# Hash bits of a masked attention kernel by three matmuls per half instead of four, with the two small parts gathered in one tile

## The chip, the cores and the metric

The kernel runs on one core of a Trainium2 chip. The metric is the device time in microseconds (us), from one launch of the program; the number given for a kernel is the median of its runs. The core has a matrix engine (TensorE, in the rows PE, with its weight loads as PEld), a vector engine (DVE), a scalar engine (ACT), GpSimd (POOL), and SP, which here issues every DMA. Each engine works through its own instructions in order and waits at an instruction until its semaphores allow it.

## What is computed

There are three stages. The first is an attention over 2 batches of 8 heads (16 heads), 768 tokens, 64 dimensions, in which a token sees only the tokens of its own hash bucket. The hash of a token has six bits, the signs of six projections of its q or k row:

```python
q_bits = (np.einsum('bhsd,dk->bhsk', q, proj) > 0).astype(np.int64)
k_bits = (np.einsum('bhsd,dk->bhsk', k, proj) > 0).astype(np.int64)
...
mask = q_bucket[:, :, :, None] == k_bucket[:, :, None, :]
scores = scale * np.matmul(q, k.transpose(0, 1, 3, 2))
scores = np.where(mask, scores, -1000000000.0)
...
return np.matmul(attn, v).astype(np.float32)
```

The other two stages are feed-forward blocks on the 1536 rows of 512 columns that the attention gives: `g = h * cos(h)`, then `g = h * tanh(softplus(h))`, each between a 512 to 2048 and a 2048 to 512 matrix.

## The kernel before

Matmuls run on float32 data that is split into a high part (rounded to the matrix engine's fp32r type) and a low part (the rest), and products of the parts are summed. For each head the tile `q2` has 128 rows: the low part of q in rows 0 to 63 and the high part in rows 64 to 127, transposed so that the 768 tokens lie along the row. `k2` is the other way round: high part in rows 0 to 63, low part below. `q1` and `k1` hold the high part in one half and, in the other half, a one-hot code of the hash bucket; so the four matmuls of a score tile (`qk`) give the scores and the mask in one sum.

**The loop.** The attention runs over turns t from -1 on. A turn is one tile of 128 queries of a head, and six turns make one head: `H1, j = divmod(t + 1, J)` with J = 6, so j is the step within the head and H1 counts heads. In a turn the program issues, in this order: the transposes of a probability tile six turns back (`pt(c, 0)`), slot 0, the score matmuls of this turn (`qk(t)`), the exponential of the turn before (`exp(t - 1)`), slot 1, the second group of transposes (`pt(c, 1)`), slot 2, four matmuls with v (`pv`), slot 3. Heads are numbered from 0.

**The slots.** While head H1 is worked on, a table called `plan` places the preparation of head H1 + 1 (and the first half of head H1 + 2) into slots (j, slot): the transposes of q and k (`setup_tr`, whose result ACT copies out of PSUM into q2 or k2), the hash bits (`setup_bits`, one call for each half of 384 tokens: four matmuls into one PSUM tile `wb`, then ACT's Sign into `sg`), and the mask (`setup_mask`: the `match` matmul of `sg` with a code table, then a DVE compare into `oh`, and after the second half two DMAs that copy `oh` into q1 and k1). Head 0 is prepared ahead of the loop in `first_head`, and head 1 has a table of its own, as it is prepared within a single head (t = -1 to 4).

**Four matmuls for the bits.** The weights `prs` hold the projection split in two parts, each for q and for k. A half's bits are q2 times the high part, q2 times the low part, k2 times the high part, k2 times the low part. Since q2 and k2 carry both parts of the data in their 128 rows, each matmul sums both.

**What goes through SP.** All DMAs are on SP's one queue, in program order: the loads of q, k, v of later heads (`load`), of the feed-forward weights (`load_w`), the copies of the high part from q2 to q1 and from k2 to k1 (line 277), of the one-hot rows (lines 302 and 303), and the shift of attention results (`sh`, line 390). Besides, eight completion semaphores are used in turn, so that a DMA is issued only after the one eight places ahead of it has landed.

**PSUM.** The tiles of the transposes, the bits and the match share a pool of three buffers (`ps_w`), the score tiles one of two (`ps_s`): a new score tile waits for the exponential of the tile two turns back.

**Work that fills gaps.** From t = 7 on `fill(j)` puts one piece of the conversion of the first four weight tiles into a turn: ACT pieces at j = 3, DVE pieces (lines 140, 142, 145) at j = 5, 0 and 1, POOL pieces at j = 2. One weight tile takes two heads, so that every second head, up to head 8, has DVE pieces at its j = 0 and j = 1.

## Time and profile before

| what | value |
|---|---|
| time, median of 3 runs | 797.54 us (796.18 to 797.77) |
| the profiled execution's own time | 796.35 us |
| its span, first to last instruction | 794.6 us |
| TensorE busy | 777.2 us (98%), 4020 matmuls |
| VectorE / ScalarE / GpSimd busy | 541.8 / 502.1 / 305.3 us |
| mean granted TensorE clock | 0.994 of full speed |

The profile is of one execution. Busy time of an engine is the time in which at least one of its instructions is recorded as running. Matmuls are pipelined, so a matmul that is recorded with 334 ns can be followed by the next after less than that: the cost of one is read from start to start. Most of the table is an average over three stages with different limits, so the rows below are cut by stage, by head and by step.

### The profile page before, as it was taken

What the parts mean: (1) busy time and instruction counts of PE and PEld (TensorE: products, weight loads), DVE (VectorE), ACT (ScalarE), POOL (GpSimd) and SP (SyncE); (2) the same over time, 40 slices, a digit from 0 to 9 for tenths busy, and PEclk for the clock granted to TensorE, in tenths of its full rate; (3) what the DMA queues carried; (4) which work ended last, traced back from release to release, by engine and by line L of the source; (5) the groups of instructions that cost most, each with busy time, mean ns of one, the idle gap of its engine ahead of it and who ended that gap; (6) DMA issues with size and microseconds to landing.
All of it is one profiled execution on the core that took longest, in us unless ns stands there. A gap on an engine that the chain in (4) does not pass through costs nothing.

```text
span 794.6 us, 11720 instructions
## 1 busy us (share of the span) xinstructions
PE 777.2 (98%) x4020; PEld 665.5 (84%) x4020; DVE 541.8 (68%) x944; ACT 502.1 (63%) x1002; POOL 305.3 (38%) x327
## 2 busy tenths in 40 slices
PE   7999999999999898999999999999999999999998
PEld 5889999999999676887888888888888888888886
DVE  5799899888897898559888546998412766611122
ACT  5899999998997786567777656875223444322120
POOL 4779999998876532102222001232200221200000
PEclk9999999999999999999999999999999999999999
DMA  8454454443320433002332001333100232001011
GB/s 230 105 153 111 105 148 120 105 110 106 85 51 20 139 108 102 30 27 79 107 106 84 23 1 55 105 106 106 54 1 27 81 105 80 1 1 54 0 54 53
DMA packets 38027, 62.36 MB, mean 78 GB/s; under 512 B 3664, under 2 KB 28368, under 8 KB 37968
## 3 DMA queue, kind: packets, MB, share of 16 engines
q1 hardware_dynamic: 37968, 61.63, 26.4%
q8 instruction: 31, 0.51, 0.3%
q14 instruction: 28, 0.23, 0.1%
HBM read 43.13 MB, written 3.15 MB: 58 GB/s over the span
## 4 chain that ended last, share of the span: by engine, by line
PE 59%; DVE 3%; ACT 1%; issue 1%; DVEq 0%; ACTq 0%
PE o L665 30%; PE h L174 29%; DVE hs L199 2%; DVE pa L641 0%; ACT gh L207 0%; ACT hs L184 0%; ACT a L186 0%; DVE gl L209 0%; ACT a L192 0%; DVE ct L142 0%; DVE cg L145 0%; DVE ct L140 0%; ACT pa L627 0%; ACT cg L131 0%; DVE pa L623 0%
## 5 line engine op out<-in xcount | busy, mean ns | idle before, releaser
L174 PE MATMUL h<-xh,w 128*128 128x512 f32 x752 | 246.7, 389 | 0.6 <-POOL xh L397 0.6
L154 POOL TENSOR_TENSOR w<-cg,w 128x512 fp32r<-128x512 f32 x64 | 88.5, 1384 | 343.1 <-ACT w L152 330.9
L209 DVE TENSOR_TENSOR gl<-hs,gh 128x512 fp32r<-128x512 f32 x96 | 69.0, 719 | 168.6 <-ACT gh L207 168.6
L174 PEld LDWEIGHTS h<-xh,w 128*128 128x128 f32 x752 | 141.2, 188 | 30.1 <-POOL xh L397 1.0
L174 PE MATMUL h<-xl,w 128*128 128x512 f32 x376 | 146.4, 389 | 2.3 <-POOL xl L400 2.3
L181 ACT ACTIVATE hs<-h 128x512 f32<-128x512 f32 x48 | 28.7, 598 | 158.7 <-PE h L174 158.7
L665 PE MATMUL o<-gh,w 128*128 128x512 f32 x384 | 120.8, 396 | 4.6 <-DVE pa L625 3.9
L367 DVE TENSOR_TENSOR pl<-wp,ph 128x384 fp32r<-128x384 f32 x192 | 105.8, 552 | 23.3 <-ACT ph L365 22.7
L665 PE MATMUL o<-w,gh 128*128 128x512 f32 x384 | 118.3, 389 | 0.0
L365 ACT ACTIVATE ph<-wp 128x384 fp32r<-128x384 f32 x192 | 95.8, 500 | 17.5 <-PE wp L361 17.4
L326 DVE TENSOR_REDUCE nm<-s 128x1 f32<-128x768 f32 x96 | 90.1, 938 | 5.3 <-PE s L324 5.3
L324 PE MATMUL s<-k,q 128*128 128x512 f32 (+1 forms) x384 | 91.6, 361 | 2.0 <-DVE k L478 1.3
L665 PEld LDWEIGHTS o<-gh,w 128*128 128x128 f32 x384 | 73.4, 192 | 21.1 <-ACT a L192 4.3
L174 PEld LDWEIGHTS h<-xl,w 128*128 128x128 f32 x376 | 70.6, 188 | 17.2 <-POOL xl L400 2.6
L665 PEld LDWEIGHTS o<-w,gh 128*128 128x128 f32 x384 | 72.1, 188 | 15.0
L665 PE MATMUL o<-gl,w 128*128 128x512 f32 x192 | 75.6, 394 | 0.0
L665 PE MATMUL o<-w,gl 128*128 128x512 f32 x192 | 74.7, 389 | 0.0
L377 PE MATMUL u<-ph,nv 128*128 128x384 f32 x192 | 72.5, 378 | 0.0
L184 ACT ACTIVATE hs<-h 128x512 f32<-128x512 f32 x46 | 27.5, 598 | 63.6 <-PE h L174 31.6
L199 DVE SCALAR_TENSOR_TENSOR hs<-hs,b 128x512 f32<-128x512 f32 x48 | 64.9, 1352 | 1.8 <-ACT b L193 1.8
L377 PE MATMUL u<-pl,nv 128*128 128x384 f32 x192 | 64.9, 338 | 0.3 <-DVE pl L367 0.3
L324 PEld LDWEIGHTS s<-k,q 128*128 128x128 f32 x384 | 58.9, 191 | 6.9 <-DVE k L478 1.5
(102 smaller groups left out, 1429.2 us busy)
## 6 DMA issues: line engine op xcount, KB each, us to landing
wr<-in_moe_w_in_dram SPq DMA_DIRECT2D x32, 512.0 KB, 3.8
wr<-in_moe_w_out_dram SPq DMA_DIRECT2D x32, 512.0 KB, 3.3
rq<-in_q_dram SPq DMA_DIRECT2D x16, 192.0 KB, 2.9
rk<-in_k_dram SPq DMA_DIRECT2D x16, 192.0 KB, 2.7
rv<-in_v_dram SPq DMA_DIRECT2D x16, 192.0 KB, 3.4
q<-q SPq DMA_DIRECT2D x16, 192.0 KB, 2.7
k<-k SPq DMA_DIRECT2D x16, 192.0 KB, 2.7
sh<-us SPq DMA_DIRECT2D x32, 96.0 KB, 2.2
```

What stands on the lines that cost most here:

```text
L154: nc.gpsimd.tensor_tensor(w[:, 1], g, f32(w[:, 0]), ALU.subtract)
L174: nc.tensor.matmul(hp, w[:, wi, c, :], X[b][c], start=(i == 0), stop=(i == 3 * NCT - 1))
L181: nc.scalar.activation(hs, hp, ACTF.Mish)
L184: nc.scalar.activation(hs, hp, ACTF.Copy, scale=INV2PI)
L199: nc.vector.scalar_tensor_tensor(hs1, hs1, TWO_PI, b1, ALU.mult, ALU.mult)
L209: nc.vector.tensor_tensor(gl, hs, f32(gh), ALU.subtract)
L324: nc.tensor.matmul(s[:, c0:c1], T[a][:, qs], T[c][:, c0:c1], start=(n == 0), stop=(n == 1))
L326: nc.vector.tensor_reduce(nm, s, AX.X, ALU.max, negate=True)
L365: nc.scalar.activation(ph, w, ACTF.Copy)
L367: nc.vector.tensor_tensor(pl, w, f32(ph), ALU.subtract)
L377: nc.tensor.matmul(U[0], lw, x, start=(kt == 0 and n == 0), stop=(kt == J - 1 and n == 1))
L665: nc.tensor.matmul(O[d], lhs, rhs, start=(first and x == 0), stop=(last and x == 2))
```

## The change

The two matmuls with the low part of the projection are replaced by one. Its moving operand is a new tile `z`, 128 rows by 768 tokens, which holds the high part of q in rows 64 to 127 and the high part of k in rows 0 to 63; its weights `prz` hold the low part of the projection for k in rows 0 to 63 and for q in rows 64 to 127. The product of the two low parts is left out. A half's bits are then q2 and k2 with the high weights, and z with `prz`. The tile z is filled by DMAs on SP, one for each side and each half of the tokens, issued right behind ACT's copy of that part; the two copies into q1 and k1 move behind them, to the place of the last one. Head 0 keeps its four matmuls.

`sg` becomes one buffer of a half's size, written by each half in turn; so the second half's bits move from slot (2, 1) to (3, 1), behind the match of the first half. For head 1 the table changes to bits at (2, 3) and (3, 2) (before: (2, 1) and (2, 3)), mask at (3, 1) and (4, 1) (before: (3, 1) and (3, 3)). `prw`, a source of the weights, takes a turn in the pool of raw weight tiles in place of a tile of its own, so that the third weight load of `first_head` also waits for the last of POOL's two new instructions that make `prz`.

```diff
-    prw = persist.tile([128, 2, 128], F32, name="prw")
     prs = persist.tile([128, 2, 2, 128], F32R, name="prs")
+    prz = persist.tile([128, 128], F32R, name="prz")
...
                 o = T[a][:, half * HF:half * HF + HF]
                 nc.scalar.activation(o, tr_unit(nat_t[h], half), ACTF.Copy, scale=sc)
+                if half == 0 and side == 0:
+                    T["z"] = oh_p.tile([128, S], F32R, tag="z", name="z")
+                cs = slice(half * HF, half * HF + HF)
+                nc.sync.dma_start(out=f32(T["z"][rows:rows + 64, cs]), in_=f32(T[a][rows:rows + 64, cs]))
                 if half == 1:
-                    nc.sync.dma_start(out=f32(T[b][64:128, :]), in_=f32(T[a][rows:rows + 64, :]))
+                    if side == 1:
+                        nc.sync.dma_start(out=f32(T["q1"][64:128, :]), in_=f32(T["q2"][64:128, :]))
+                        nc.sync.dma_start(out=f32(T["k1"][64:128, :]), in_=f32(T["k2"][0:64, :]))
                     nat_t.pop(h)
...
-                for i, (x, nm, part) in enumerate((x, nm, part) for x, nm in enumerate(("q2", "k2")) for part in range(2)):
-                    nc.tensor.matmul(w, prs[:, part, x, :], T[nm][:, cs], start=(i == 0), stop=(i == 3))
-                if half == 0:
-                    T["sg"] = oh_p.tile([128, S], F32R, tag="sg", name="sg")
-                nc.scalar.activation(T["sg"][:, cs], w, ACTF.Sign, bias=tiny, scale=1.0)
+                if h:
+                    ws = ((prs[:, 0, 0, :], "q2"), (prs[:, 0, 1, :], "k2"), (prz, "z"))
+                else:
+                    ws = [(prs[:, part, x, :], nm) for x, nm in enumerate(("q2", "k2")) for part in range(2)]
+                for i, (lw, nm) in enumerate(ws):
+                    nc.tensor.matmul(w, lw, T[nm][:, cs], start=(i == 0), stop=(i == len(ws) - 1))
+                if h or half:
+                    sg = oh_p.tile([128, HF], F32R, tag="sg", name="sg")
+                else:
+                    sg = p_p.tile([128, S], F32, tag="p7", name="sg0")[:, 0:HF].bitcast(F32R)
+                T["sg", half] = sg
+                nc.scalar.activation(sg, w, ACTF.Sign, bias=tiny, scale=1.0)
...
+                nc.gpsimd.tensor_tensor(prz[0:64, :], prw[0:64, 1], f32(prs[0:64, 0, 1]), ALU.subtract)
+                nc.gpsimd.tensor_tensor(prz[64:128, :], prw[64:128, 0], f32(prs[64:128, 0, 0]), ALU.subtract)
...
-                        (1, 1): lambda: setup_bits(h, 0), (2, 1): lambda: setup_bits(h, 1),
+                        (1, 1): lambda: setup_bits(h, 0), (3, 1): lambda: setup_bits(h, 1),
...
-                        (2, 1): lambda: setup_bits(h, 0), (2, 3): lambda: setup_bits(h, 1),
-                        (3, 1): lambda: setup_mask(h, 0), (3, 3): lambda: setup_mask(h, 1),
+                        (2, 3): lambda: setup_bits(h, 0), (3, 2): lambda: setup_bits(h, 1),
+                        (3, 1): lambda: setup_mask(h, 0), (4, 1): lambda: setup_mask(h, 1),
```

Where the change moves instructions is seen best in an engine's list. The first place is SP's queue at the start of the loop, where head 1 is prepared. Before, from the last of the loads that `first_head` and the first turn issue (`rq`, `rk`, `rv`: q, k, v of later heads) to the one-hot copies of head 1 (`q_263`, `k_265` are q1 and k1 of head 1, `q_264`, `k_266` its q2 and k2; DMAHW0 to 7 are the eight completion semaphores):

```order
L247 DMA rq<-in_q_dram 128x384 [waits DMAHW0_49,Pool_49]
L247 DMA rk<-in_k_dram 128x384 [waits DMAHW1_49,Pool_49]
L247 DMA rv<-in_v_dram 128x384 [waits DMAHW2_49,Pool_49]
L277 DMA q_263<-q_264 64x768 [waits DMAHW3_49,Activation_49]
L277 DMA k_265<-k_266 64x768 [waits DMAHW4_49,Activation_49]
L302 DMA q_263<-oh 64x768 [waits DMAHW5_49,DVE_49]
L303 DMA k_265<-oh 64x768 [waits DMAHW6_49]
```

The same place now (`q_267`, `k_269` are q1 and k1 of head 1, `q_268`, `k_270` its q2 and k2):

```order
L247 DMA rq<-in_q_dram 128x384 [waits DMAHW0_49,Pool_49]
L247 DMA rk<-in_k_dram 128x384 [waits DMAHW1_49,Pool_49]
L247 DMA rv<-in_v_dram 128x384 [waits DMAHW2_49,Pool_49]
L279 DMA z<-q_268 64x384 [waits DMAHW3_49,Activation_49]
L279 DMA z<-k_270 64x384 [waits DMAHW4_49,Activation_49]
L279 DMA z<-q_268 64x384 [waits DMAHW5_49,Activation_49]
L279 DMA z<-k_270 64x384 [waits DMAHW6_49,Activation_49]
L282 DMA q_267<-q_268 64x768 [waits DMAHW7_49]
L283 DMA k_269<-k_270 64x768 [waits DMAHW0_49]
L315 DMA q_267<-oh 64x768 [waits DMAHW1_49,DVE_49]
L316 DMA k_269<-oh 64x768 [waits DMAHW2_49]
```

Four transfers into z stand between the loads and the copies; the copies of the high part and of the one-hot rows come four places later.

The second place is TensorE in the same stretch, from the second score tile of head 0 on. Before (`s` are score tiles, `wb` the bits, `wm` the match; `q_264` and `k_266` are q2 and k2 of head 1):

```order
L324 MATMUL s<-k_183,q_181 128x256
L285 MATMUL wb<-q_264,prs 128x384 [waits Activation_49]
L285 MATMUL wb<-q_264,prs 128x384
L285 MATMUL wb<-k_266,prs 128x384 x2
L285 MATMUL wb<-q_264,prs 128x384 [waits Activation_49]
L285 MATMUL wb<-q_264,prs 128x384
L285 MATMUL wb<-k_266,prs 128x384 [waits Activation_49]
L285 MATMUL wb<-k_266,prs 128x384
L324 MATMUL s<-k_182,q_180 128x512 [waits Activation_49]
```

Now, at the same place:

```order
L337 MATMUL s<-k_186,q_184 128x256
L295 MATMUL wb<-q_268,prs 128x384 [waits Activation_49]
L295 MATMUL wb<-k_270,prs 128x384
L295 MATMUL wb<-z,prz 128x384 [waits DMAHW4_49,DMAHW3_49]
L337 MATMUL s<-k_185,q_183 128x512 [waits Activation_49]
L337 MATMUL s<-k_185,q_183 128x256
L337 MATMUL s<-k_186,q_184 128x512
L337 MATMUL s<-k_186,q_184 128x256
L305 MATMUL wm<-sg,code 128x384 [waits Activation_49]
L295 MATMUL wb<-q_268,prs 128x384 [waits PE_49]
L295 MATMUL wb<-k_270,prs 128x384
L295 MATMUL wb<-z,prz 128x384 [waits DMAHW6_49,DMAHW5_49]
```

The third matmul of each half now waits for two transfers into z, and the third score tile of head 0 stands behind the first of these waits; the second half's bits stand behind that score tile and the first match.

The third place is TensorE in a later head, at j = 2 and j = 3. Before, from the score tile of j = 2 on, the second half's bits stand at j = 2, ahead of the second transposes (`wp`):

```order
L324 MATMUL s<-k_2347,q_2345 128x256
L285 MATMUL wb<-q_2642,prs 128x384 [waits Activation_49]
L285 MATMUL wb<-q_2642,prs 128x384
L285 MATMUL wb<-k_2644,prs 128x384 x2
L361 MATMUL wp<-con,hs 128x128 [waits DVE_49]
```

Now they stand one step later, behind the score tile of j = 3, and j = 2 has none:

```order
L337 MATMUL s<-k_2383,q_2381 128x256
L295 MATMUL wb<-q_2682,prs 128x384 [waits DVE_49]
L295 MATMUL wb<-k_2684,prs 128x384
L295 MATMUL wb<-z,prz 128x384 [waits DMAHW1_49,DMAHW0_49]
L374 MATMUL wp<-con,hs 128x128 [waits DVE_49]
```

Each half has one matmul less, and the first waits on DVE, through the PSUM buffer that it takes over, where it waited on ACT.

## Rows read from the trace of the kernel before

**Rows 1.** Windows: us; busy PE, PEld, DVE, ACT, POOL (instructions); clock; DMA share, GB/s.

```profile
0.00:24.14 24.14, 18.81 (x104) 14.20 (x104) 11.55 (x25) 13.84 (x28) 14.06 (x26) 0.93 0.76 210
57.85:238.90 181.05, 181.05 (x1274) 171.12 (x1272) 165.30 (x398) 167.38 (x390) 163.82 (x192) 1.00 0.41 107
```

**Rows 2.** Timeline of TensorE, one step of head 10: start, us, operation.

```profile
163.21 0.94 PE L324 MATMUL s<-k,q 128*128 128x512 f32 x4
163.99 0.51 PE L285 MATMUL wb<-q,prs 128*128 128x384 f32 x2
...
164.69 0.27 PE L361 MATMUL wp<-con,hs 128*128 128x128 f32 x1
...
178.27 0.48 PE L324 MATMUL s<-k,q 128*128 128x512 f32 x1
```

**Rows 3.** Busy time by engine of two heads, from j = 2 to j = 2; columns as Rows 1.

```profile
103.01:118.06 15.05, 15.05 (x109) 14.24 (x108) 13.98 (x35) 14.18 (x33) 14.88 (x19) 1.00 0.54 141
...
163.21:178.27 15.06, 15.06 (x110) 14.27 (x108) 13.33 (x33) 13.70 (x33) 13.84 (x18) 1.00 0.40 107
```

**Rows 4.** Single steps: j = 1, 2, 3 with conversion pieces, then j = 2 without.

```profile
130.36:133.11 2.75, 2.75 (x21) 2.59 (x19) 2.75 (x7) 2.64 (x7) 2.75 (x4) 1.00 0.71 164
133.11:136.04 2.93, 2.93 (x22) 2.78 (x21) 2.93 (x8) 2.63 (x6) 2.93 (x4) 1.00 0.91 268
136.04:138.27 2.23, 2.23 (x18) 2.11 (x17) 2.23 (x6) 1.89 (x5) 2.23 (x4) 1.00 0.51 177
...
178.27:181.20 2.93, 2.93 (x22) 2.77 (x21) 2.27 (x6) 2.64 (x6) 2.17 (x3) 1.00 0.64 221
```

**Rows 5.** Timeline of DVE: one conversion piece in those steps.

```profile
133.80 0.68 DVE L145 SCALAR_TENSOR_TENSOR cg<-cg,ct 128x512 int32<-128x512 int32 x1
```

**Rows 6.** Loads of line 247 at 11.2 to 13.3 us: last issue, time to landing.

```profile
L247 SPq DMA_DIRECT2D rv<-in_v_dram x1: 459/459/459, 12.8 to 12.8; - x1
...
DMA to landing us min/median/max: 7.9/8.3/8.6
```

**Rows 7.** Copies of line 277 at 14.9 to 17 us: issues, time to landing.

```profile
L277 SPq DMA_DIRECT2D q<-q x1: 467/467/467, 15.0 to 15.0; - x1
L277 SPq DMA_DIRECT2D k<-k x1: 467/467/467, 16.4 to 16.4; - x1
...
DMA to landing us min/median/max: 6.5/6.8/7.2
```

**Rows 8.** The last one-hot copy of head 1, line 303: issue, time to landing.

```profile
L303 SPq DMA_DIRECT2D k<-oh x1: 589/589/589, 18.3 to 18.3; - x1
...
DMA to landing us min/median/max: 5.6/5.6/5.6
```

**Rows 9.** Timeline of TensorE while head 1 is prepared.

```profile
13.34 0.51 PE L285 MATMUL wb<-q,prs 128*128 128x384 f32 x2
...
21.50 1.61 PE L324 MATMUL s<-k,q 128*128 128x512 f32 x4
...
24.14 1.03 PE L324 MATMUL s<-k,q 128*128 128x512 f32 x4
```

**Rows 10.** DMA issues by kind: count, KB, median us to landing.

```profile
sh<-us SPq DMA_DIRECT2D x32, 96.0 KB, 2.2
...
k<-oh SPq DMA_DIRECT2D x15, 192.0 KB, 3.0
```

**Rows 11.** Timelines of ACT and TensorE: k2's first half of a head, then its bits.

```profile
172.98 0.52 ACT L275 ACTIVATE k<-wt 128x384 fp32r<-128x384 f32 x1
...
176.28 0.34 PE L285 MATMUL wb<-q,prs 128*128 128x384 f32 x1
```

**Rows 12.** Busy time by engine at 22 to 26 us; columns as Rows 1.

```profile
22.00:26.00 4.00, 4.00 (x24) 3.73 (x23) 1.98 (x5) 3.45 (x9) 3.79 (x6) 0.71 0.32 68
```

**Rows 13.** Groups of instructions: busy us, mean ns of one, idle time before.

```profile
L326 DVE TENSOR_REDUCE nm<-s 128x1 f32<-128x768 f32 x96 | 90.1, 938 | 5.3 <-PE s L324 5.3
...
L298 DVE TENSOR_SCALAR oh<-wm,con 128x384 fp32r<-128x384 f32 x30 | 20.0, 668 | 0.0
```

More of the change, by code (lines that the diff above doesn't have):

```diff
@@ L283, in setup_bits @@
                 w = ps_w.tile([128, HF], F32, tag="w", name="wb")
-                for i, (x, nm, part) in enumerate((x, nm, part) for x, nm in enumerate(("q2", "k2")) for part in range(2)):
-                    nc.tensor.matmul(w, prs[:, part, x, :], T[nm][:, cs], start=(i == 0), stop=(i == 3))
-                if half == 0:
-                    T["sg"] = oh_p.tile([128, S], F32R, tag="sg", name="sg")
-                nc.scalar.activation(T["sg"][:, cs], w, ACTF.Sign, bias=tiny, scale=1.0)
+                if h:
[10 more added lines that the diff above has]
+                nc.scalar.activation(sg, w, ACTF.Sign, bias=tiny, scale=1.0)
             def match(h, half):
                 w = ps_w.tile([128, HF], F32, tag="w", name="wm")
-                nc.tensor.matmul(w, code, tt[h]["sg"][:, half * HF:half * HF + HF])
+                nc.tensor.matmul(w, code, tt[h]["sg", half])
                 return w
@@ L426, in attention @@
             nc.vector.memset(warm, 0.0)
+            prw = raw_p.tile([128, NCT, 128, 2], I32, tag="w", name="prw").bitcast(F32)[:, 0].rearrange("p (x f) t -> p x (f t)", x=2)
             nc.gpsimd.memset(prw, 0.0)
```

## Prediction

> **What bounds the kernel now.** I cut the table of windows by stage first. The reader is to see two attention stages, not one. From 57.85 to 238.90 us TensorE is recorded as busy in all of 181.05 us at full clock; up to 24.14 us it is busy for 18.81 us only, while the DMA engines are busy for 0.76 of the time [rows 1]. So the long stretch is bound by TensorE, and the start by something else.
>
> Whether a busy TensorE is one that works without a stall is read from its timeline, by starts. In head 10 a score tile starts at 163.21 us and the one six turns later at 178.27 us [rows 2], a period of 15.05 us that the two heads shown share to 0.01 us [rows 3]; the four matmuls of a half's bits take from 163.99 to 164.69 us [rows 2], 0.175 us each from start to start. Nothing in that is a wait.
>
> The other engines have little room in the same period. In a head with conversion pieces DVE is busy for 13.98 and ACT for 14.18 of 15.05 us, and POOL for 14.88 us; later, without pieces, 13.33, 13.70 and 13.84 us [rows 3]. Cut by step it is tighter: from j = 1 to j = 3 of a head with pieces DVE has no idle time at all (2.75, 2.93 and 2.23 us busy of as much), where the same j = 2 without pieces leaves it 0.66 us of 2.93 [rows 4]. The piece of line 145 alone is 0.68 us [rows 5].
>
> Then the start, in SP's queue. The loads issued from 11.3 to 12.8 us land 7.9 to 8.6 us later, so the last one, of v, at 12.8 + 8.6 = 21.4 us [rows 6]. What is issued behind lands behind: the copy q2 to q1 of head 1 goes out at 15.0 and lands 7.2 us later at 22.2, that of k2 goes out at 16.4 and lands 6.5 us later at 22.9 [rows 7], and the last one-hot copy goes out at 18.3 and lands 5.6 us later at 23.9 [rows 8]. The first score tile of head 1 starts at 24.14 us [rows 9], right behind it. But the hash bits of head 1 ran already from 13.34 us on [rows 9]: they needed no transfer, and the mask, the score tiles of head 0 and the one-hot copies were all done or issued while the queue emptied. That is the cover which I look at below.
>
> **What the change removes.** One matmul for each half of heads 1 to 15: 30 in all. For head 1 it falls into a stretch in which TensorE waits anyway. For the 14 others it is 2 x 0.175 = 0.35 us of a period of 15.05, at most 14 x 0.35 = 4.9 us. At the other bound it is nothing, where another engine sets the pace of the steps. Which it is I take head by head. DVE does the same work as before. In the heads with pieces at j = 0 and j = 1 (heads 2, 4, 6 and 8, four of the fourteen) it is busy through j = 1, 2 and 3 without a break [rows 4], and its lead or lag against TensorE is held by three PSUM buffers; the bits at j = 2 were the time in which it caught up, and they move away. There I take no gain. In the other ten DVE was idle for 0.66 us in j = 2 [rows 4], and 0.70 us of bits now comes one step later, at j = 3, where 0.52 us of it is left; so it loses no room ahead of the tight steps, and I take the full 0.35. Sum: 10 x 0.35 = 3.5 us, with bounds of 1.75 (half of that, if a new wait appears in every second head) and 4.9.
>
> **What it adds to a steady head.** Four transfers of 96 KB. One of that size lands in 2.2 us by the median [rows 10]. The closest is k's first half: ACT's copy out of PSUM ends at 172.98 + 0.52 = 173.50, and the bits start at 176.28 [rows 11], the third matmul 0.35 us later; 173.50 + 0.47 for the issue (the duration of such an issue in [rows 7]) + 2.2 is 176.2, so 0.45 us are left. If it landed as the slower copies do, in 3.0 us [rows 10], TensorE would lose 0.35 us per head, all of the gain. I cost it at nothing, since the size is that of the 2.2 us row. The copies into q1 and k1 go out later, but are read a step and more later than the one-hot copies; the queue time of four issues (4 x 0.47 = 1.9 us of 15) leaves SP waiting most of the time. POOL's two small instructions, and the third weight load's wait on them, come ahead of the loop, where POOL has the loads still to wait for that land up to 21.4 us [rows 6]; without that cover they would cost less than 1 us, once.
>
> **What it adds at the start.** Here the cover is gone. The four transfers into z for head 1 stand behind the loads that land up to 21.4 us [rows 6]. Two copies of 192 KB land 0.7 to 0.8 us apart there [rows 7], so a transfer of half the size takes some 0.4 us: the first two, which the first half's bits need, have landed at 21.4 + 2 x 0.4 = 22.2 us. TensorE works in order. It reaches that third matmul at 13.34 + 0.35 = 13.7 us and waits there for 8.5 us; queued behind are the third to sixth score tile of head 0, the matches, and the transposes for head 2, none of which needs z. Followed on:
> - 22.2: third matmul. TensorE's clock will be low after this idle time: before, at 22 to 26 us, the granted clock was 0.71 on average, that is partly at 1.2 GHz, after shorter gaps, and a score tile at 21.50 took 1.61 us [rows 12, 9] where one takes 0.94 [rows 2]. So the bits end at 22.5 and the next score tile's last matmul near 24.1.
> - Then the first match and the second half's three matmuls, at about 0.35 us each at the low clock as far as it lasts: 24.9.
> - The next score tile, whose buffer must have been read by an exponential that stood behind the first Sign, 0.94 and some latency: 25.9. Its maximum on DVE, which stands ahead of the second half's mask, 0.94, and the mask 0.67 [rows 13]: 27.5.
> - The two one-hot copies, issued 0.47 us apart [rows 7]; the second lands 3.0 us after its issue [rows 10], in a queue that is now empty: 31.0.
>
> Head 1's first score tile then starts at 31.05 instead of 24.14: a loss of 6.9 us, that nothing gives back, since TensorE is the bound behind it. Bounds: with the full clock throughout 0.7 (a score tile) and 0.7 (bits and match) go away, 5.5; with the low clock for two more score tiles 1.1 come on top, 8.0.
>
> **The sum.** 6.9 - 3.5 = 3.4 us more than the profiled execution's own 796.35 (794.6 of span and 1.75 around it): 799.75. That execution is 1.2 us below the median of the three runs; taking half of that gives 800.4 us.
>
> **Rivals.**
> - *The start costs nothing (faster).* TensorE waited in this stretch before too, for POOL and ACT, and ended with the one-hot copies at 23.9; if the transfers into z from SBUF overtook the loads, or the rest of head 1's preparation fitted into the old waits, only the gain is left: 796.35 - 3.5 to - 4.9, near 792.5. It decides from the point where z's first half lands before 15 us. Against it: all of four copies issued there landed behind the loads, in order [rows 6 to 8].
> - *z pays its own duration only.* If a transfer took 2.2 us [rows 10] from its issue, as one into an empty queue, the second would go out at 16.4 [rows 7], land at 18.6, and the chain above would end 3.6 us earlier: a loss of 3.3, and with the gain of 3.5 a time of 796.2, no change. The copies of the same place, with 6.5 and 7.2 us, speak against it. The Trainium skill (DMA: Bandwidth & Descriptors, Anatomy of one DMA) gives a fixed 2.0 us and the bytes at 436 GB/s for each DMA, a fit from GpSimd's path; for 96 KB that is an estimate of 2.2 us, which the 2.2 us of [rows 10] bears out and the start does not.
> - *Another engine takes the whole gain.* POOL's 14.88 us in a head [rows 3] is more than the new period of 14.70, or z comes late at j = 1 in each head (0.35 us each, above). Then the loss stands alone: 796.35 + 6.9, near 803.3. Against it: POOL's work in the other heads is 13.84, and its results are used turns later.
>
> **How the numbers follow.** My forecast, a start that costs 5.5 to 8.0 and a gain of 1.75 to 4.9, has 0.67; the first rival 0.14, the second 0.11, the third 0.08. The forecast's own range is 796.35 + 0.6 to + 6.25, with up to 1.2 for the median: 797.0 to 803.8. For 8 in 10 I go from 796.2 to 803.8, which takes in the second rival and leaves out the first and some of the third. About 0.2% (1.6 us) is what a measurement can tell from no change: slower than that is most of the forecast (0.58 of its 0.67) and the third rival, 0.66; the same is the rest of the forecast and most of the second rival, 0.19; faster is the first rival and a little of the second, 0.15.
>
> **What would show it.** Right: TensorE idle for some 8 us up to 22 us, ended by a DMA into z; head 1's first score tile near 31 us; then periods of 14.70 us, with about 15.05 in heads 2, 4, 6 and 8; the end of the attention 3 to 4 us later. Wrong: z landing ahead of the loads; a first score tile of head 1 before 27 us; periods that are not shorter in the heads without pieces; or waits for z at j = 1 of every head.

## The result and the profile after

The changed kernel takes 802.58 us, the median of 5 runs (800.26 to 803.64), against 797.54 us: the ratio is 1.0063 with a 95% interval of 1.0041 to 1.0084. It is slower, by about 5 us (0.6%). The profiled execution took 803.14 us (span 801.3, granted clock 0.989); the one of the kernel before took 796.35 us (span 794.6). TensorE has the 30 matmuls less (3990) and is busy for 775.7 us. The line numbers are those of the changed kernel now: 337 the score tile, 295 the bits, 305 the match, 279 the copies into z.

The start answers to [rows 9]. The timeline of TensorE while head 1 is prepared (start, us, operation, idle time before it and what ended it; rows left out are marked with dots):

```profile
13.55 0.34 PE L295 MATMUL wb<-q,prs 128*128 128x384 f32 x1
13.73 0.33 PE L295 MATMUL wb<-k,prs 128*128 128x384 f32 x1
21.26 0.66 PE L295 MATMUL wb<-z,prz 128*128 128x384 f32 x1 [7.20 <-DMA z<-k]
21.71 1.48 PE L337 MATMUL s<-k,q 128*128 128x512 f32 x4
...
24.27 1.45 PE L337 MATMUL s<-k,q 128*128 128x512 f32 x4
...
31.11 0.47 PE L337 MATMUL s<-k,q 128*128 128x512 f32 x1 [1.52 <-DMA k<-oh]
```

The first two matmuls of the bits run where they ran before; the third stands for 7.20 us until z has landed. Head 1's first score tile comes at 31.11 us, 6.97 us later than in [rows 9]. 0.2 us of that were there before the preparation: head 0's first score tile came at 11.25 us, in the profile before at 11.05.

SP's queue answers to [rows 6, 7]. The last load, and the four copies into z (issues, then the time from issue to landing):

```profile
L247 SPq DMA_DIRECT2D rv<-in_v_dram x1: 432/432/432, 13.0 to 13.0; - x1
...
DMA to landing us min/median/max: 7.4/7.4/7.4
```

```profile
L279 SPq DMA_DIRECT2D z<-q x2: 468/508/547, 15.0 to 17.0; - x2
L279 SPq DMA_DIRECT2D z<-k x2: 467/512/558, 16.4 to 17.6; - x2
...
DMA to landing us min/median/max: 4.2/4.6/5.8
```

The load issued at 13.0 lands at 20.4. The first copy into z lands at 15.0 + 5.8 = 20.8 and the last at 17.6 + 4.2 = 21.8, in order behind it; the second, which completes the first half of z, lands at 21.1.

The heads and steps answer to [rows 1, 3, 4]. Windows of the changed kernel: the stretch that was all TensorE, then head 10, then j = 1, 2 and 3 of head 4 (with conversion pieces), then j = 3 of head 5 (without); columns as Rows 1.

```profile
57.85:238.90 181.05, 180.01 (x1262) 167.02 (x1261) 164.99 (x399) 168.62 (x395) 167.74 (x197) 1.00 0.53 137
167.54:182.25 14.71, 14.71 (x107) 13.78 (x106) 13.24 (x32) 13.56 (x34) 14.04 (x17) 1.00 0.53 135
...
77.05:79.64 2.59, 2.59 (x20) 2.42 (x19) 2.59 (x7) 2.56 (x6) 2.59 (x4) 1.00 0.51 116
79.64:81.97 2.33, 2.33 (x18) 2.04 (x17) 2.33 (x7) 2.13 (x5) 2.33 (x4) 1.00 0.95 278
81.97:85.16 3.19, 3.05 (x22) 2.52 (x20) 3.19 (x8) 2.58 (x6) 3.19 (x4) 1.00 0.90 237
...
97.10:99.88 2.78, 2.78 (x22) 2.51 (x20) 2.78 (x8) 2.44 (x6) 2.78 (x4) 1.00 0.45 131
```

Head 10 has a period of 14.71 us, as forecast. But TensorE is no longer recorded as busy all the time: in head 4 the step from 81.97 us (j = 3), which now holds the second half's bits, takes 3.19 us where the same step of head 5 takes 2.78. All periods, first score tile to first score tile, for the kernels that matter below (us, good to 0.01; each from the timeline of its one profiled execution; the kernels of the last three columns are those of the next section):

| head | before | changed | head 1 old | bits at j = 2 | pieces moved |
|---|---|---|---|---|---|
| 1 | 14.87 | 14.73 | 16.61 | 17.00 | 14.67 |
| 2 | 16.07 | 16.38 | 16.37 | 16.07 | 15.39 |
| 3 | 15.07 | 14.83 | 14.87 | 14.90 | 14.97 |
| 4 | 15.04 | 15.22 | 15.24 | 14.98 | 14.77 |
| 5 | 15.05 | 14.73 | 14.72 | 14.83 | 14.98 |
| 6 | 15.05 | 15.12 | 15.16 | 14.98 | 14.71 |
| 7 | 15.06 | 14.73 | 14.92 | 15.31 | 15.88 |
| 8 | 15.04 | 15.97 | 15.99 | 15.37 | 14.71 |
| 9, 10 | 15.06, 15.05 | 14.72, 14.71 | 14.70, 14.73 | 14.75, 14.74 | 14.70, 14.72 |
| 11, 12 | 15.06, 15.05 | 14.92, 14.72 | 14.71, 14.73 | 14.75, 14.73 | 14.70, 14.73 |
| 13, 14 | 15.06, 14.12 | 14.71, 13.81 | 14.71, 13.77 | 14.75, 13.79 | 15.56, 13.77 |

From head 1 to head 14 the changed kernel wins 1.33 us in all, not 3.5. From head 2 on TensorE never waits for z in this execution.

Two more places cost time. In head 8 POOL stood idle ahead of the addition that needs the transfer `sh`; that transfer, issued at 142.3 us, landed 5.4 us later, at 147.6, right behind a weight load of 512 KB that was issued ahead of it:

```profile
L403 SPq DMA_DIRECT2D sh<-us x1: 467/467/467, 142.3 to 142.3; - x1
...
DMA to landing us min/median/max: 5.4/5.4/5.4
```

```profile
147.71 1.01 POOL L407 TENSOR_TENSOR xt<-us,sh 64x384 f32<-64x384 f32 x1 [1.89 <-DVE pl L380]
148.68 0.99 POOL L257 TENSOR_TENSOR nk<-rk,nk 128x384 fp32r<-128x384 f32 x1
```

```profile
149.73 0.45 PE L263 MATMUL wt<-ident_r,nk 128*128 128x128 f32 x3 [0.62 <-POOL nk L257]
```

The view names DVE as what ended POOL's wait, since a `pl` ended at the same moment. But the addition starts 0.07 us behind the landing, as the additions of heads 2, 4 and 6 that wait for `sh` do, so the landing is what it waited for. Behind the addition stands k's low part, and TensorE waits for that: the step takes 3.15 us instead of 2.29. In the kernel before, the `sh` of the same place took 4.7 us too and cost nothing: it went out 3.7 us behind the head's first score tile, and now 5.4 us behind it. So most of the delay is the later issue.

And behind the attention TensorE's granted clock is 0.50 (the 1.2 GHz level) for twice as long. First the kernel before at that place, then the changed kernel:

```profile
300.81:304.23 3.42, 3.13 (x8) 2.49 (x9) 3.28 (x7) 1.85 (x4) 0.09 (x1) 0.50 0.05 12
```

```profile
305.46:312.28 6.82, 5.54 (x13) 4.41 (x14) 6.67 (x10) 3.22 (x6) 1.60 (x1) 0.50 0.27 83
```

The lag against the kernel before grows there from 5.64 to 6.76 us. So the profiled executions add up: 6.97 (start) - 1.33 (heads) + 1.1 (clock) = 6.7 us, the difference of the two spans.

### The profile page after: what moved, and what is told of

Its sections match the earlier page's. It is cut to its first block, busy times and chain, and to the rows that moved or that the text cites. A ratio compares the mean times of both kernels' runs of the same rounds, so it can differ in the third digit from the quotient of the medians.

```text
span 801.3 us, 11825 instructions
## 1 busy us (share of the span) xinstructions
PE 775.7 (97%) x3990; PEld 660.6 (82%) x3990; DVE 541.8 (68%) x944; ACT 501.4 (63%) x1002; POOL 305.3 (38%) x329
## 3 DMA queue, kind: packets, MB, share of 16 engines
HBM read 43.13 MB, written 3.15 MB: 58 GB/s over the span
## 4 chain that ended last, share of the span: by engine, by line
PE 59%; DVE 3%; ACT 1%; issue 1%; DVEq 0%; ACTq 0%
PE o L681 30%; PE h L174 29%; DVE hs L199 2%; DVE pa L657 0%; ACT gh L207 0%; ACT hs L184 0%; ACT a L186 0%; DVE gl L209 0%; ACT a L192 0%; DVE ct L142 0%; DVE cg L145 0%; DVE ct L140 0%; ACT pa L643 0%; ACT cg L131 0%; DVE pa L639 0%
## 5 line engine op out<-in xcount | busy, mean ns | idle before, releaser
L184 ACT ACTIVATE hs<-h 128x512 f32<-128x512 f32 x46 | 27.5, 598 | 64.8 <-PE h L174 32.8
```

The source lines that it names most:

```text
L184: nc.scalar.activation(hs, hp, ACTF.Copy, scale=INV2PI)
```

## The experiments

Times are medians; "before" is the kernel before, measured beside each group on the same chip: 797.09 us beside the first four kernels, 797.72 us beside the next seven, 797.97 us beside the last. The first eight kernels ran on one chip, the next three on a second and the last on a third, so across these groups the ratios are the better measure. Each kernel was profiled in one execution. Only the lines of an edit that matter most are shown; the same condition also switches the transfers into z.

**Head 1 as before, the rest changed.**

```diff
-                if h:
+                if h and not (h == 1):
                     ws = ((prs[:, 0, 0, :], "q2"), (prs[:, 0, 1, :], "k2"), (prz, "z"))
...
-                        (2, 3): lambda: setup_bits(h, 0), (3, 2): lambda: setup_bits(h, 1),
-                        (3, 1): lambda: setup_mask(h, 0), (4, 1): lambda: setup_mask(h, 1),
+                        (2, 1): lambda: setup_bits(h, 0), (2, 3): lambda: setup_bits(h, 1),
+                        (3, 1): lambda: setup_mask(h, 0), (3, 3): lambda: setup_mask(h, 1),
```

> The changed kernel, but head 1 is prepared as before: four matmuls for each half, the old places in its table, no transfers into z for it. My theory (the start costs 6.9 us because z of head 1 waits behind the loads, and everything else is worth -1.3 us): head 1's first score tile starts at 24.1 us again, the heads keep the periods of the changed kernel (14.7, and 15.1 to 15.4 in heads 2, 4, 6 and 8), and the time is 795.0, or up to 796.2 if the second stretch at the low clock behind the attention lasts 6.8 us here too. Rival (the 6.9 us are not lost through z but turn up wherever the queue is held back): first score tile at 24.1, but the lag comes back within heads 1 to 3, and the time is 800 or more.

Measured: 796.1 us (795.20 to 798.13), ratio to before 0.9983 (0.9971 to 0.9996), so 6.5 us below the changed kernel. Head 1's first score tile starts at 24.35 us, and from head 2 to head 14 the periods are those of the changed kernel within about 0.2 us (third column of times). Only head 1 itself lost 1.7 us against the kernel before, and not through the queue: the clock stayed at 0.50 for 6.8 us there:

```profile
22.24:29.06 6.82, 6.31 (x27) 5.34 (x26) 3.51 (x8) 4.75 (x11) 5.24 (x7) 0.50 0.76 203
```

In the profile before, the low clock lasted 3.4 us there, from 20.92; the kernel with the pieces moved, further down, has the same start, no low clock at all there, and 14.67 us for head 1. So the 6.9 us sit in the preparation of head 1, and the rest of the change is worth a little more than 1 us.

**Only head 1 changed.**

```diff
-                if h:
+                if h and not (h > 1):
                     ws = ((prs[:, 0, 0, :], "q2"), (prs[:, 0, 1, :], "k2"), (prz, "z"))
...
-                        (1, 1): lambda: setup_bits(h, 0), (3, 1): lambda: setup_bits(h, 1),
+                        (1, 1): lambda: setup_bits(h, 0), (2, 1): lambda: setup_bits(h, 1),
```

> Only head 1 has the three matmuls, the transfers into z and the new places; heads 2 to 15 have four matmuls, the bits of both halves at j = 1 and j = 2, and the copies where they were. My theory: head 1's first score tile at 31.1, then 15.05 us per head as before, so the time is 796.35 + 6.9 = 803.3. Rival (the lag of the start is given back later, since buffers are fuller or DVE has caught up): below 800.

Measured: 804.81 us (803.52 to 804.95), ratio 1.0081 (1.0064 to 1.0099). The third matmul waits 7.07 us for z and head 1's first score tile starts at 31.65:

```profile
21.70 0.66 PE L298 MATMUL wb<-z,prz 128*128 128x384 f32 x1 [7.07 <-DMA z<-k]
31.65 0.59 PE L344 MATMUL s<-k,q 128*128 128x512 f32 x2 [1.60 <-DMA k<-oh]
```

The lag is 7.52 us at head 1 (0.76 of it are there at head 0's first score tile already) and 7.57 at the last score tile: nothing is given back. Another 1.0 us comes behind the attention, again with 6.8 us at the low clock; that and the later start of head 0 make up most of what this execution took above the 803.3 us that I expected.

**The move alone: four matmuls, second half's bits at j = 3.**

```diff
-                if h:
+                if h and not (h > 0):
                     ws = ((prs[:, 0, 0, :], "q2"), (prs[:, 0, 1, :], "k2"), (prz, "z"))
```

> Four matmuls in every head and no z; only the place of the second half's bits is the new one (j = 3 instead of j = 2) and sg has one half's size; head 1 has its old table. My theory (in heads 2, 4, 6 and 8 the moved bits wait for DVE, which has no idle time from j = 1 to j = 3): heads without conversion pieces keep 15.05 us, heads 2, 4, 6 and 8 take some 0.2 us more, since TensorE comes there 0.17 us later than with three matmuls; time 796.35 + 0.8 = 797.2. Rival (the stall at j = 3 belongs to z, whose last transfer lands too late for the second half): no stall, 15.05 us in every head, 796.4.

Measured: 799.07 us (796.16 to 802.54), ratio 1.0029 (1.0010 to 1.0047). Heads 6 and 8 take 15.21 us each, heads 5, 7 and 9 to 14 what they took before: 0.16 us more, about the theory's 0.2, and no z is there to cause it. The total is more than forecast, since heads 1 to 4 lose 3.7 us in the profiled execution; 2.4 of that lies in heads 3 and 4, where DVE's conversion pieces ran beside other POOL work (last section).

**Second half's bits back at j = 2, with three matmuls.**

```diff
-                        (1, 1): lambda: setup_bits(h, 0), (3, 1): lambda: setup_bits(h, 1),
+                        (1, 1): lambda: setup_bits(h, 0), (2, 1): lambda: setup_bits(h, 1),
...
-                    sg = oh_p.tile([128, HF], F32R, tag="sg", name="sg")
+                    sg = oh_p.tile([128, HF], F32R, tag="sg", name="sg", bufs=2)
```

> Three matmuls and z from head 2 on, head 1 as before, and the second half's bits at j = 2 as before, with two sg buffers of half size (the low projection weights of heads 0 and 1 stand in a probability tile that is not yet in use). My theory (the move to j = 3 makes the stalls in heads 2, 4, 6 and 8): these heads take 14.9 to 15.05 us, the others 14.7, and the time is 796.35 - 3.3 to - 4 = 792.4 to 793.0, or a microsecond more if the low clock behind the attention lasts as in the changed kernel. Rival (DVE is short in these heads wherever the bits stand): the same stalls of 0.4 us, and the time of the kernel that has only head 1 as before.

Measured: 796.76 us (793.95 to 798.34), ratio 0.9983 (0.9967 to 0.9998): the same as with the bits at j = 3. I had expected 792.4 to 793.0, and missed. Both theories have a part of it. Heads 4 and 6 go from 15.2 to 14.98 us, so the move does cost 0.2 us there; but they don't reach 14.7, and heads 7 and 8 now take 15.3 to 15.4 us. In the profile the low clock of the start, 6.8 us again, takes 2.1 us more of head 1 than in the kernel before (17.00 against 14.87 us).

**The weight loads issued later.** The three loads of 512 KB that `first_head` puts into SP's queue go to three turns of the loop. This edit was tried on the changed kernel, on the kernel before, and on the one with head 1 as before:

```diff
-                for _ in range(3):
-                    load_w()
...
+                if t in (4, 10, 16):
+                    load_w()
```

> The changed kernel with one more edit: the three weight loads of 512 KB that stand ahead of head 1's loads in SP's queue are issued later, one each at t = 4, 10 and 16. My theory (z of head 1 takes 5 to 6 us since it lands behind 1.5 MB of weights and the loads after them): the transfers into z land some 2.2 us after their issue, the third matmul of the first half starts near 18.7 instead of 21.3, head 1's first score tile near 28.4 instead of 31.1, and the time is 2.7 us less than the changed kernel's 802.6: near 800. Rival (the transfers within SBUF are slow there by themselves, or the wait is for POOL): third matmul at 21.3 as before, 802.6.

Measured on the changed kernel: 796.5 us (795.25 to 797.65), 6 us less, ratio to before 0.9985 (0.9975 to 0.9996). The direction was right and the size twice what I expected: SP issues a DMA only after the one eight places ahead has landed, which for the first two copies into z were weight loads (landed at 14.91 and 16.37, copies issued at 14.97 and 16.43), so that without these the copies also go out 1.7 to 2.6 us earlier. The copies into z, and TensorE:

```profile
L279 SPq DMA_DIRECT2D z<-q x2: 467/506/546, 13.3 to 14.5; - x2
L279 SPq DMA_DIRECT2D z<-k x2: 547/547/547, 13.8 to 15.1; - x2
...
DMA to landing us min/median/max: 2.1/2.2/2.5
```

```profile
16.12 0.41 PE L295 MATMUL wb<-z,prz 128*128 128x384 f32 x1 [1.84 <-DMA z<-k]
...
24.80 0.47 PE L337 MATMUL s<-k,q 128*128 128x512 f32 x1 [1.83 <-DMA k<-oh]
```

They land in 2.1 to 2.5 us instead of 4.2 to 5.8. That is the transfer's own time, and the wait shrinks from 7.20 to 1.84 us. The queue is shown as the cause of most of the wait.

> The kernel before with the same edit of the weight loads and nothing else. My theory: its last one-hot copy of head 1, which landed 5.6 us after its issue, lands in about 3.0 us, but TensorE waits in that stretch for POOL too (the transposes of k of head 2 started at 21.1 behind a wait for POOL), so that head 1's first score tile comes 0.5 to 2.5 us earlier than 24.1; time 796.6 to 794.6. Rival (the queue was hidden in the kernel before, POOL alone sets the end of head 0): 24.1 and no change.

Measured on the kernel before: 795.75 us (794.55 to 796.82), ratio 0.9982 (0.9971 to 0.9992). Head 1's first score tile starts at 22.43 instead of 24.14. The queue was not fully hidden there either. Against this kernel, the changed one with late loads is still 2.4 us behind at that tile and 0.75 us slower by the medians. No run separates what of that is z's own transfer and what the later places of head 1's bits and masks.

> Head 1 prepared as before (four matmuls, no z), the rest as in the changed kernel, and the three weight loads issued at t = 4, 10 and 16. My theory: the saving of the kernel that has only head 1 as before (1.3 us of periods against the kernel before, some of it lost to a longer stretch at the low clock at the start) and that of the late loads add up: 0.5 to 2.5 us less than without late loads, 793.5 to 795.5. Rival (POOL alone sets the end of head 0): the time of the kernel with only head 1 as before, 796.1.

Measured with head 1 as before: 794.48 us (792.99 to 794.84), ratio 0.9963 (0.9951 to 0.9975); first score tile at 22.00. The two savings add up: 0.9983 times 0.9982 is 0.9965.

**DVE's pieces moved.** Head 1 as before, and:

```diff
-            SLOTS = {"A": (3,), "D": (0, 1, 5), "P": (2,)}
+            SLOTS = {"A": (3,), "D": (0, 4, 5), "P": (2,)}
```

> Head 1 prepared as before, the rest as in the changed kernel, and DVE's conversion pieces moved from j = 5, 0 and 1 to j = 4, 5 and 0. My theory (in heads 2, 4, 6 and 8 TensorE waits at j = 3 for DVE, which has no idle time from j = 0 to j = 3 there, while j = 4 leaves it 0.6 us): heads 4 and 6 take 14.7 instead of 15.1 to 15.2 us, head 8 keeps its other stall of 0.8 us if that is the queue's; time about 1.2 us below the kernel with only head 1 as before, near 795. Rival (the stall at j = 3 comes from the later bits themselves): heads 4 and 6 stay at 15.1 to 15.2 us, 796.1.

Measured: 795.3 us (794.01 to 797.8), ratio 0.9975 (0.9960 to 0.9991). Heads 4, 6 and 8 take 14.77, 14.71 and 14.71 us: the step with the second half's bits is 2.77 us in heads 6 and 8, as in heads without pieces. The stall belonged to DVE. The pieces have a smaller price at their new place: heads 3, 5 and 7 take 0.25 us more at j = 0, as they do in the kernel before with both edits below. The time itself is not clear of that without the move (0.9983, 0.9971 to 0.9996), and its profile also lacked the low clock at the start, which is worth 1.9 us of head 1; the argument rests on the steps. Head 8's other stall went too; its weight load now stands one step earlier in the queue. New ones appeared in head 7 (15.88 us) and head 13 (15.56), where k's first half of z was late; head 7:

```profile
L280 SPq DMA_DIRECT2D z<-k x1: 461/461/461, 112.0 to 112.0; - x1
...
DMA to landing us min/median/max: 3.9/3.9/3.9
```

```profile
115.96 0.44 PE L298 MATMUL wb<-z,prz 128*128 128x384 f32 x1 [0.64 <-DMA z<-k]
```

**Both edits together,** on three kernels: with head 1 as before, on the whole change, and on the kernel before.

> Head 1 as before, three matmuls from head 2 on, the three weight loads issued at t = 4, 10 and 16, and DVE's conversion pieces at j = 4, 5 and 0: the two edits together. My theory (the queue of the start and DVE in heads 2, 4, 6 and 8 are separate places): head 1's first score tile near 22, heads 4, 6 and 8 at 14.7 to 14.8 us, time near 793 (794.5 of the kernel with late loads, less some 1.5 of stalls). Rival (transfers into z that land late now and then give the rest back): some heads with a stall of 0.6 to 0.9 us at j = 0, and 794.5.

> The whole change, head 1 included, with the late weight loads and the pieces at j = 4, 5 and 0. My theory: the transfers into z of head 1 still put 2 us into the start even with the queue empty (24.8 instead of 22.0 for head 1's first score tile with late loads), so the time is some 2 us above the same kernel with head 1 as before: near 795. Rival (with the queue empty z costs nothing): equal to it, 793.

> The kernel before, four matmuls and old places, with the same two edits: late weight loads, pieces at j = 4, 5 and 0. My theory (the kernel before has no wait for DVE in heads 4, 6 and 8, only some in head 2): 0 to 1 us below the kernel before with late loads alone, 794.8 to 795.8; so that three matmuls from head 2 on, with head 1 as before, are worth 1.8 to 2.8 us in the same surroundings. Rival (the edits, not the three matmuls, made the faster times): the same time as with three matmuls, 793.

Measured: 793.57 us (792.87 to 794.9; ratio 0.9948, 0.9930 to 0.9965), 795.41 us (793.37 to 799.04; ratio 0.9971, 0.9953 to 0.9989), and 795.31 us (794.61 to 795.68; ratio 0.9973, 0.9965 to 0.9982). The first is the fastest kernel of the study, 0.5% below the kernel before. In the same surroundings three matmuls from head 2 on are worth 795.31 - 793.57 = 1.7 us (the two intervals just touch), and taking head 1 into the change costs 1.8 us even with the queue empty (first score tile at 24.58 instead of 22.77). The intervals of the first and the second of these kernels overlap, but the tile says the same. So the whole change with both edits is no faster than the kernel before with both edits.

In the first, the rival had a part too. Heads 7 and 13 keep their late z (15.95 and 15.31 us), head 4 did not come down (15.23 us; TensorE waits for `pl` again), and in head 2 (16.51 us) a z that was queued behind two of the late weight loads held TensorE up:

```profile
45.17 0.41 PE L298 MATMUL wb<-z,prz 128*128 128x384 f32 x1 [0.91 <-DMA z<-k]
```

**The first half's bits later,** on the fastest kernel:

```diff
-                        (1, 1): lambda: setup_bits(h, 0), (3, 1): lambda: setup_bits(h, 1),
+                        (1, 3): lambda: setup_bits(h, 0), (3, 1): lambda: setup_bits(h, 1),
```

> The kernel with head 1 as before, late weight loads and pieces at j = 4, 5 and 0, and now the first half's bits behind the v matmuls of j = 1 instead of ahead of the second transposes there. My theory (single transfers into z land 3.5 to 4.3 us after their issue instead of 2.1, and where that is k's first half TensorE waits 0.6 to 1.2 us at the bits of j = 1, as in heads 7 and 13): the bits come some 0.8 us later, heads 7 and 13 lose 0.1 us or nothing, and the time is about 1 us less than without this edit, near 792.5. Rival (the first half's sign and match are then late, and TensorE waits at the match of j = 2 in every head): each head takes 0.1 us more, 795 or above.

Measured: 796.64 us (793.57 to 797.91), ratio 0.9978 (0.9962 to 0.9993). The rival won, though through another wait than it named. The late z of head 7 no longer costs anything (15.41 us), but from head 3 to head 14 every step with the second half's bits takes 3.17 to 3.19 us. The waits of these twelve heads (who waited for whom, us in total, times, longest), then, in head 10, where no piece is near, DVE and TensorE:

```profile
PEld wb L298 <- DVE pl L383: 5.4, 12, 0.5
```

```profile
164.49 0.94 DVE L342 TENSOR_REDUCE nm<-s 128x1 f32<-128x768 f32 x1
165.35 0.55 DVE L383 TENSOR_TENSOR pl<-wp,ph 128x384 fp32r<-128x384 f32 x1
```

```profile
164.87 0.94 PE L340 MATMUL s<-k,q 128*128 128x512 f32 x4
165.95 0.45 PE L298 MATMUL wb<-q,prs 128*128 128x384 f32 x1
```

The bits start right behind DVE's `pl`, which ends at 165.90 and sets free the PSUM buffer.

## Why the prediction was right, and where it was off

**The bound, and the cover at the start: right.** TensorE's order, the transfers into z behind the loads, and what stands behind the third matmul came as forecast. So did the steady heads' transfers into z, which I had costed at nothing: TensorE never waited for one there. Step by step: the two transfers of the first half landed at 21.1 us (forecast 22.2), the first half's bits then released TensorE, the last but two of head 0's score tiles ended at 25.7 (25.9), the one-hot copies were issued from 27.3 on (mask at 27.5), and head 1's first score tile came at 31.11 (31.05). The two early steps were off by about a us in opposite ways: the loads were in a little sooner, and the clock was at 0.50 up to 25.6 us, the whole stretch and not a part of it. The loss was 6.97 us, forecast 6.9. That the two came out so close is partly luck, since these errors cancelled. The kernel with only head 1 changed and the one with only head 1 unchanged show the loss from both sides, and late weight loads show the cause. The Trainium skill (DMA: Bandwidth & Descriptors, Two DMAs through the same engine are not ordered) says that descriptors within one queue of one engine start in order but are pipelined, and that nothing orders DMAs across the 16 engines. In the profile of the changed kernel all 27 transfers issued up to 28 us landed in their order of issue.

**The second rival's own time of a transfer** was the right price for an empty queue: 2.1 to 2.5 us with the weights out of the way. It was not the price here, with 4.2 to 5.8, and that rival also took the time of issue (16.4) for given, which the weights had set as well.

**The gain: right in kind, mis-sized.** "10 x 0.35 = 3.5 us, with bounds of 1.75 and 4.9" measured 1.33, below the lower bound. The ten heads without pieces gave 2.8 us; seven of them 0.31 to 0.34 us each, and heads 1, 3 and 11 only 0.13 to 0.24. The step that failed is "There I take no gain" for heads 2, 4, 6 and 8: they don't stay at zero but lose 0.31, 0.18, 0.07 and 0.93 us. I had reasoned that DVE's lag is held by three PSUM buffers, and that the bits at j = 2 were its time to catch up; I did not follow where TensorE meets DVE next. It meets it at the moved bits, which take over the buffer that `pl` reads. In head 4 of the changed kernel, DVE, then TensorE, then what the wait for the bits' weights was put down to:

```profile
82.47 0.54 DVE L380 TENSOR_TENSOR pl<-wp,ph 128x384 fp32r<-128x384 f32 x1
```

```profile
83.06 0.44 PE L295 MATMUL wb<-q,prs 128*128 128x384 f32 x1
```

```profile
PEld wb L295 <- DVE pl L380: 0.5, 1, 0.5
```

And in head 5, without pieces:

```profile
97.18 0.55 DVE L380 TENSOR_TENSOR pl<-wp,ph 128x384 fp32r<-128x384 f32 x1
```

```profile
97.88 0.34 PE L295 MATMUL wb<-q,prs 128*128 128x384 f32 x1
```

The `pl` of head 4 starts 0.50 us behind the score tile of 81.97, and the bits start as it ends; in head 5 it starts 0.08 us behind (97.18 against 97.10), and the bits follow the score tile with no gap. Moving the pieces removed the stall of 0.4 us; the move alone, with four matmuls, made 0.16 us of it; putting the bits back gave heads 4 and 6 14.98 us, a gain of 0.07, close to the zero that I had forecast.

**What was not in the sum.** The stall of head 8 (0.86 us) goes through a queue that I had costed at nothing: four more transfers a head and the later copies put `sh` 1.7 us later into the queue, behind a weight load, and it then took 5.4 us where it took 4.7 before. And 1.1 us of low clock behind the attention, which comes and goes between executions: of the twelve kernels of the experiments, eight show 6.8 us of it there in their profile and four 3.4. Why it varies was not settled, but since the kernel before took from 795.12 to 800.53 us in 29 runs on one chip (with a granted clock of 0.989 in the slowest and 0.995 in the fastest), a difference of some us between two single executions means little.

**The range held** since the two misses, 2.2 us of missing gain and 1.1 us of clock, stayed within what I had left for the other cases: 799.75 + 2.2 + 0.1 + 1.1 = 803.1, the profiled execution. The gain itself fell outside its own bounds, so that the total stayed inside is partly luck.

**The third rival** was closer than its chance of 0.08: another engine (DVE) and the queue took 2.2 of the 3.5 us, though in some heads and not in all. What I had set against it, POOL's spare time, was not the point.

## What to carry to other kernels

Replacing a matmul's operand that stands in place by one that a DMA must first gather moves the start of that matmul to the end of the queue: cost the first use by what was issued ahead of it, here 2.1 to 2.5 us in an empty queue against 4.2 to 5.8 behind 1.5 MB of prefetch and six more loads, and prefetch behind the first use. A matmul that is taken out of a TensorE-bound loop pays only where the next engine has room at the place at which TensorE meets it again (here the PSUM buffer three tiles on); moving work to a later step changes that place. Leave the first iteration, which has no cover, in its old form: that alone turned 5 us of loss into a gain of about 1 us.

## What the runs showed of the hardware

**DVE and POOL hold each other up.** One conversion piece of line 145, with two inputs in SBUF, behind POOL's addition (head 2) and ahead of POOL's scaling (head 4), in the changed kernel; first DVE, then POOL:

```profile
49.76 1.32 DVE L145 SCALAR_TENSOR_TENSOR cg<-cg,ct 128x512 int32<-128x512 int32 x1
...
80.47 0.68 DVE L145 SCALAR_TENSOR_TENSOR cg<-cg,ct 128x512 int32<-128x512 int32 x1
```

```profile
49.53 1.01 POOL L257 TENSOR_TENSOR nq<-rq,nq 128x384 fp32r<-128x384 f32 x1
...
80.56 1.36 POOL L359 TENSOR_SCALAR a<-a,r 128x768 f32<-128x768 f32 x1
```

At 49.76 POOL is at work until 50.54, and the piece takes 1.32 us instead of 0.68; at 80.47 the piece is first, and POOL's scaling takes 1.36 us instead of 0.90. The Trainium skill (SBUF — State Buffer, Who interferes with whom) says that a DVE instruction with two SBUF inputs contends with a GpSimd instruction that reads SBUF, that the port pair they share is an exclusive lock, and that the order of issue decides who blocks. These rows agree. Not every row is as clear: in the kernel with the move alone a piece of line 140, which has one input, took 1.61 us beside POOL's 1.30 us for `xl`, and 0.41 us in two later heads beside 1.5 us for the same `xl`, though POOL's record begins 0.03 to 0.04 us behind the piece's each time; TensorE waited 0.8 us behind the slow one. So the same pieces cost their price or several times that, and a small shift in time seems to decide which.

**Single transfers into z land late, and two rows go with it.** In the nine kernels that use z from head 2 on, 478 transfers into z were issued after 24 us. 391 landed within 2.55 us (the median is near 2.1), 87 later, up to 7.3 us. The 50 transfers that were issued while a weight load of 512 KB was still on its way ahead of them were all late. Of the other 37, the 33 that took over 3.1 us all had a packet of 16 KB on the queue that the DMA view calls `instruction` in their way: it started 0.5 to 1.8 us behind the issue and took 0.9 to 1.6 us. Of the 391, none had one that started between 0.2 and 1.5 us behind the issue. A late transfer and a normal one of the changed kernel, issued at 102.6 and 87.9 us (queue, packets, MB, share of the 16 engines; then KB, us to landing):

```profile
q1 hardware_dynamic: 286, 0.47, 51.4%
q8 instruction: 1, 0.02, 1.8%
...
z<-q SPq DMA_DIRECT2D x1, 96.0 KB, 3.5
```

```profile
q1 hardware_dynamic: 277, 0.46, 56.1%
...
z<-q SPq DMA_DIRECT2D x1, 96.0 KB, 2.1
```

The late z of head 7 in the kernel with the pieces moved, issued at 112.0, is such a case as well. These packets come near the same places of the program in different executions, which fits the late transfers' doing so. No run moved the packets, so that they are the cause is argued, not shown.
